# Exponentials of pairs of tiles in two places by turns, and weight blocks taken up two tiles behind their load: a fused attention and feed-forward kernel on one core

## The chip, the cores and the metric

The kernel runs on one core of a Trainium2 chip. A core has five engines that run side by side and wait for each other by semaphores: TensorE (PE in the profile; its weight loads are PEld), VectorE (DVE), ScalarE (ACT), GpSimd (POOL) and SyncE (SP), which here issues all transfers. Each engine works through its instructions in a fixed order. The metric is the device time of one launch in microseconds; the kernel before took 1450.28 us (median of three runs, 1449.85 to 1451.96).

## The reference

```python
scores = scale * np.matmul(q, k.transpose(0, 1, 3, 2))          # q, k, v: (8, 8, 576, 64)
thresh = np.max(scores, axis=-1, keepdims=True) - tau
scores = np.where(scores >= thresh, scores, -1000000000.0)
attn = np.exp(scores - np.max(scores, axis=-1, keepdims=True))
attn = attn / (np.sum(attn, axis=-1, keepdims=True) + 1e-09)
x = np.matmul(attn, v)                                           # -> (4608, 512), heads side by side
h = x @ w_in                                                     # w_in (512, 2048)
g = np.maximum(h, 0.0) + np.log1p(np.exp(-np.abs(h)))            # softplus
out = g @ w_out                                                  # w_out (2048, 512)
```

All inputs are 32-bit floats, tau is a scalar of 0.02.

## The kernel before

**Attention in units of nine tiles.** A unit is a pair of heads of one batch: 32 units, of 2 x 576 = 1152 query rows each. Its nine tiles have 128 queries by 576 keys: tiles 0 to 3 are of the first head, 5 to 8 of the second, and tile 4 (called M or `NC` in the code) takes 64 rows of each. For one tile PE makes the scores in one of two pairs of PSUM banks (`scores`, line 423); DVE takes the row maximum, negated (`row_max`, line 430), and a threshold (line 431); ACT writes the exponentials to SBUF (`exps`, line 435); DVE puts zeros where the score is under the threshold and sums the rows (`mask`, line 440); PE transposes the result (`weights_T`, lines 471, 474, 477); ACT copies the transposes to gH (`weights_hi`, lines 498 to 514); and PE multiplies them with v (`values`, lines 549 to 557).

**The place of the exponentials.** They stand in `e_all`, of two halves of 576 columns, which tiles use by turns through the whole program (`nth[0] % 2`). 576 is four blocks of 128 and a rest of 64. Tiles go in pairs, 0 and 1, 2 and 3, 5 and 6, 7 and 8 (`mate`), with tile 4 alone; at the second of a pair one transpose, line 471, takes the rests of both tiles at once, the last 64 columns of the left half and the first 64 of the right half. Line 474 has the four blocks, line 477 the rest of the lone tile.

**The first units and the rest.** The first five units (`NF`, `whole`) multiply with v in full 32-bit products and have no low parts of the weights, so the buffers of tag gL stand unused there; the others split the weights in a high part gH and a low part gL. For the first 36 tiles (`TG`) transposes go to PSUM banks of their own, and the steps of a tile stand in the order `PAT0`, later in the order `PAT`, with letters for row maximum (R), exponential (e), mask (M or m), transposes (T), copies (h, l), scores (S), FFN products (f), weight blocks (w), other steps (x, v) and a count (p). `p` stands twice in each, so a tile counts two points, and `defer(n, ...)` puts a step off by n points. This order is a priority: a scheduler sets each engine's order from it and from a model of when inputs will be there, so instructions can stand earlier or later than the letters say.

**The feed-forward part (FFN).** Nine chunks of 512 tokens follow behind attention: `hidden` (lines 645, 647, 649), softplus on ACT, `project` (lines 703, 705, 707). Its first chunk needs the output of the first units, so the first 36 tiles have no FFN products beside them; after that they are strewn between the steps of attention.

**The weight blocks.** Each of 32 blocks of w_in and w_out is loaded once (SP, line 185), as words of 64 bits from which a 32-bit float is put together: an absolute value with a scale on ACT (line 193), a clamp on POOL (line 194), a shift and two "or"s on DVE (lines 200, 202, 205), and a high and a low part on POOL (lines 125, 132); parts of w_in are stored to DRAM again (SP, line 234). A block begins every second tile from tile 1. `later_(WD, first)` puts ACT's step off by WD points from the load.

Of the kernel before, what the change touches and what calls it, by code (L numbers as in the profile page):

```python
# [9 lines left out]
F32 = mybir.dt.float32  # L10
F32R = mybir.dt.float32r
# [12 lines left out]
P = 128  # L24
# [8 lines left out]
LAG0 = 5  # L33
PAT = "ThRlefmpfxSvwp"
PAT0 = "RMTeShlfpfxvwp"
WD = 2
ST = (1, 3, 4, 4, 5, 6, 6, 8)
VO = (1, 1, 1, 0)
RT = 1
# [20 lines left out]
def tile_kernel(ctx: ExitStack, tc: tile.TileContext, q, k, v, tau, w_in, w_out, out):  # L60
# [8 lines left out]
    nc = tc.nc  # L69
    B, H, S, D = q.shape  # L70
    NT, DM = out.shape
    DFF = w_in.shape[1]
    SM = 512
    SR = S - SM
    HS = S // 2
    NC = SM // P
# [8 lines left out]
    apool = ctx.enter_context(tc.tile_pool(name="apool", bufs=2))  # L85
# [11 lines left out]
    ident = identr.bitcast(F32)  # L97
# [52 lines left out]
    def to_f32(src, want, name, then):  # L150
# [29 lines left out]
        if src.dtype == F32:  # L180
            nc.sync.dma_start(m, src)
            later_(WD, lambda: then(parts, w, done))
            return
# [29 lines left out]

        later_(WD, first)

# [59 lines left out]
    for b in range(B):  # L275
        for kind in (("one", "two") if b < NSPLIT else ("all",)):
            for hp in range(NPAIR):
                s = Unit()
# [5 lines left out]
                for g, (j, members) in enumerate(groups):  # L284
                    c = 0
# [113 lines left out]

    e_all = cpool.tile([P, 2, S], F32, name="e_all")
    banks = [ps_s.tile([P, 2, 512], F32, tag="s", name=f"s_{i}") for i in range(SB)]
    nth = [0]

    def scores(s, t):
        if t == s.tiles[0]:
            s.sums = apool.tile([P, 9], F32, tag="sums", name=f"sums_{s.i}")
            s.half, s.sp, s.m, s.grp = {}, {}, {}, {}
        sp = banks[nth[0] % SB]  # L410
        s.half[t] = half = nth[0] % 2
        nth[0] += 1
        s.sp[t] = sp
        if t == NC:
            parts = [(qm[:, n, j, :], j) for j in range(2) for n in range(2)]
        else:
            j = 0 if t < NC else 1
            c = t if t < NC else t - NC - 1
            parts = [(s.qT[j][n][:, c * P:(c + 1) * P], j) for n in range(2)]
        k0 = (1 - half) * SR  # L420
        for m, (lhs, j) in enumerate(parts):
            for hf in range(2):
                i = nc.tensor.matmul(sp[:, hf, 0:HS], lhs, s.kT[j][:, k0 + hf * HS:k0 + (hf + 1) * HS],  # L423
                                     start=(m == 0), stop=(m == len(parts) - 1))
        scored.append(i)
# [6 lines left out]
        s.m[t] = (negm, thr)  # L432

    def exps(s, t):
        nc.scalar.activation(e_all[:, s.half[t], :].rearrange("p (h n) -> p h n", h=2), s.sp[t][:, :, 0:HS],  # L435
                             AF.Exp, bias=s.m[t][0], scale=1.0)

    def mask(s, t):
        e2 = e_all[:, s.half[t], :].rearrange("p (h n) -> p h n", h=2)
        masked.append(nc.vector.scalar_tensor_tensor(  # L440
            out=e2, in0=s.sp[t][:, :, 0:HS], scalar=s.m.pop(t)[1], in1=e2, op0=ALU.is_ge, op1=ALU.mult,
            accum_out=s.sums[:, s.tiles.index(t):s.tiles.index(t) + 1]))
# [8 lines left out]
    def mate(s, t):  # L451

        if t == NC:
            return None, False
        u = t if t < NC else t - 1
        return (t + 1, False) if u % 2 == 0 else (t - 1, True)

    def weights_T(s, t):
        half = s.half[t]
        e = e_all[:, half, :]  # L460
        other, second = mate(s, t)
        lone = other is None
        if 9 * NPAIR * s.b + 9 * s.hp + t < TG:
            main = ps_g.tile([P, NC, P], F32, tag="g", name=f"tm_{s.i}_{t}")
            rest = ps_g.tile([P, NC, P], F32, tag="g", name=f"tr_{s.i}_{t}")[:, 0, :] if lone or second else None
        else:
            sp = s.sp[t]
            main = sp[:, 0, :].rearrange("p (c n) -> p c n", n=P)
            rest = sp[:, 1, 0:P]
        if second:  # L470
            nc.tensor.transpose(rest, e_all.rearrange("p h n -> p (h n)")[:, SM:SM + P], ident)  # L471
        for c in range(NC):
            c0 = half * SR + c * P
            nc.tensor.matmul(main[:, c, :], e[:, c0:c0 + P], ident, is_transpose=True, start=True, stop=True)  # L474
        if lone:
            r0 = 0 if half else SM
            nc.tensor.transpose(rest[0:SR, :], e[:, r0:r0 + SR], ident)
        s.sp[t] = (main, rest)
# [358 lines left out]
    for kind, g in WL:  # L837
        for m in range(4):
            n = len(prep)
# [71 lines left out]
    for n in (0, 2, 1):  # L911
        qkT(u0, 1, n)
        point()
    u0.eng, u0.eng_lo = eng, nc.gpsimd
    scores(*tiles[0])
    row_max(*tiles[0])
    exps(*tiles[0])
    scores(*tiles[1])
    for j in range(2):
        split_v(u0, j)  # L920
# [3 lines left out]
    for g, (cur, t) in enumerate(tiles):  # L924
# [5 lines left out]
        for step in PAT0 + ("m" if g == TG - 1 else "") if g < TG else PAT:  # L930
            if step == "T":
                weights_T(cur, t)
            elif step == "h":
                weights_hi(cur, t)
            elif step == "l":
                weights_lo(cur, t)
            elif step == "R" and nxt:
                row_max(*nxt)
            elif step == "e" and nxt:
                exps(*nxt)  # L940
            elif step == "m" and nxt:
                mask(*nxt)
            elif step == "M":
                mask(cur, t)
            elif step == "f":
                upto += quota / PAT.count("f")
                while done < upto:
                    done += next(ffn)
            elif step == "x":
                extras(cur.i, cur.tiles.index(t))  # L950
            elif step == "S" and g + 2 < NS:
                scores(*tiles[g + 2])
            elif step == "v":
                slow_products()
            elif step == "w":
                while prep and prep[0][0] <= g:
                    _, f, a = prep.pop(0)
                    f(*a)
            elif step == "p":
                point()  # L960
# [38 lines left out]
```

## Time and profile before

| | |
|---|---|
| median of 3 runs | 1450.28 us (1449.85 to 1451.96) |
| the profiled execution | 1450.65 us, span 1448.9 us |
| PE busy | 1399.3 us, 97% of the span |
| DVE busy | 983.1 us, 68% |
| ACT busy | 848.1 us, 59% |
| POOL busy | 591.0 us, 41% |
| mean granted PE clock | 0.994 |

The shares are means over stages that differ: PE is not full in the first tenth of the span and almost full after it. An engine's idle time is written beside the instruction that came after it, with what ended it. Idle time on an engine that nobody waits for costs nothing.

### The profile page before, as it was taken

What the parts mean: (1) busy time and instruction counts of PE and PEld (TensorE: products, weight loads), DVE (VectorE), ACT (ScalarE), POOL (GpSimd) and SP (SyncE); (2) the same over time, 40 slices, a digit from 0 to 9 for tenths busy, and PEclk for the clock granted to TensorE, in tenths of its full rate; (3) what the DMA queues carried; (4) which work ended last, traced back from release to release, by engine and by line L of the source; (5) the groups of instructions that cost most, each with busy time, mean ns of one, the idle gap of its engine ahead of it and who ended that gap; (6) DMA issues with size and microseconds to landing.
All of it is one profiled execution on the core that took longest, in us unless ns stands there. A gap on an engine that the chain in (4) does not pass through costs nothing.

```text
span 1448.9 us, 23497 instructions
## 1 busy us (share of the span) xinstructions
PE 1399.3 (97%) x7860; PEld 1161.6 (80%) x7860; DVE 983.1 (68%) x2211; ACT 848.1 (59%) x1615; POOL 591.0 (41%) x619
## 2 busy tenths in 40 slices
PE   6987999999999999999999999999999999999998
PEld 4654788878888888888888888888888888788886
DVE  6977688877777777777777777777777777402111
ACT  5766767767656566657665665667665765311010
POOL 3667666544333333344334333444334431324221
PEclk9999999999999999999999999999999999999999
DMA  5767765445333533444433533354344532344321
GB/s 160 220 192 231 212 187 170 138 121 154 109 102 110 137 115 110 119 134 150 123 111 96 153 106 101 116 151 120 113 119 136 148 98 74 101 130 129 119 85 44
DMA packets 131208, 189.93 MB, mean 131 GB/s; under 512 B 35312, under 2 KB 86800, under 8 KB 131088
## 3 DMA queue, kind: packets, MB, share of 16 engines
q1 hardware_dynamic: 131088, 188.43, 44.5%
q8 instruction: 63, 1.03, 0.3%
q14 instruction: 57, 0.47, 0.1%
HBM read 140.51 MB, written 27.41 MB: 116 GB/s over the span
## 4 chain that ended last, share of the span: by engine, by line
PE 78%; DVE 7%; ACT 5%; issue 3%; DMA 3%; POOL 2%; SPq 1%; POOLq 0%; ACTq 0%; DVEq 0%
PE s L423 10%; PE h L647 9%; PE h L645 9%; PE h L649 8%; PE o L707 8%; PE o L705 7%; PE s L474 7%; PE o L703 7%; PE pv L555 3%; PE pv L556 3%; PE tr L364 2%; DVE e_all L440 2%; DVE negm L430 2%; PE pv L549 1%; POOL g L132 1%
## 5 line engine op out<-in xcount | busy, mean ns | idle before, releaser
L132 POOL TENSOR_TENSOR g<-st,g 128x512 fp32r<-128x512 f32 x144 | 191.7, 1349 | 196.3 <-DVE g L129 182.5
L440 DVE SCALAR_TENSOR_TENSOR e_all<-s,thr,e_all 128x576 f32<-128x576 f32 x288 | 234.4, 815 | 53.0 <-ACT e_all L435 49.8
L430 DVE TENSOR_REDUCE negm<-s 128x1 f32<-128x576 f32 x288 | 217.1, 754 | 43.1 <-PE s L423 34.6
L435 ACT ACTIVATE e_all<-s,negm 128x576 f32<-128x576 f32 x288 | 215.9, 751 | 39.3 <-PE tr L471 20.7
L707 PE MATMUL o<-wo_o,g 128*128 128x512 f32 x576 | 232.3, 404 | 5.3 <-POOL g L132 5.3
L703 PE MATMUL o<-wo_o,g 128*128 128x512 f32 x576 | 232.0, 403 | 1.1 <-ACT st L667 0.7
L647 PE MATMUL h<-xl,wi 128*128 128x512 f32 x576 | 232.8, 404 | 0.0
L645 PE MATMUL h<-xh,wi 128*128 128x512 f32 x576 | 229.8, 399 | 0.0
L649 PE MATMUL h<-xh,wi 128*128 128x512 f32 x576 | 229.3, 398 | 0.0
L705 PE MATMUL o<-wo_o,g 128*128 128x512 f32 x576 | 228.5, 397 | 0.0
L498 ACT CAST gH<-s 128x512 fp32r<-128x512 f32 (+1 forms) x270 | 145.0, 550 | 139.1 <-PE s L474 135.6
L132 DVE TENSOR_TENSOR gL<-s,gH 128x512 fp32r<-128x512 f32 (+1 forms) x270 | 168.8, 634 | 47.8 <-ACT gH L498 25.3
L423 PE MATMUL s<-kT,qT 128*128 128x288 f32 x1024 | 192.2, 310 | 6.2 <-ACT gH L498 1.8
L423 PEld LDWEIGHTS s<-kT,qT 128*128 128x128 f32 x1024 | 148.5, 190 | 27.9 <-issue 11.3
L474 PE MATMUL s<-identr,e_all 128*128 128x128 f32 x1008 | 155.1, 276 | 4.8 <-DVE e_all L440 4.8
L129 DVE CAST g<-st 128x512 fp32r<-128x512 f32 x128 | 57.4, 485 | 149.5 <-ACT st L667 149.0
L667 ACT ACTIVATE st<-h 128x512 f32<-128x512 f32 x144 | 78.3, 596 | 115.3 <-PE h L649 114.6
L474 PEld LDWEIGHTS s<-identr,e_all 128*128 128x128 f32 x1008 | 114.7, 141 | 22.3 <-DVE e_all L440 12.6
L707 PEld LDWEIGHTS o<-wo_o,g 128*128 128x128 f32 x576 | 108.4, 188 | 29.1 <-POOL g L132 11.0
L645 PEld LDWEIGHTS h<-xh,wi 128*128 128x128 f32 x576 | 108.3, 188 | 23.5 <-issue 1.0
L703 PEld LDWEIGHTS o<-wo_o,g 128*128 128x128 f32 x576 | 108.5, 188 | 22.2 <-DVE g L129 2.0
L649 PEld LDWEIGHTS h<-xh,wi 128*128 128x128 f32 x576 | 108.4, 188 | 21.6
(107 smaller groups left out, 2366.4 us busy)
## 6 DMA issues: line engine op xcount, KB each, us to landing
wi<-wi_d SPq DMA_DIRECT2D x144, 512.0 KB
qT<-qT SPq DMA_DIRECT2D x124, 128.0 KB
R<-r_d SPq DMA_DIRECT2D x64, 144.0 KB
kn<-in_k_dram SPq DMA_DIRECT2D x32, 256.0 KB
qn<-in_q_dram SPq DMA_DIRECT2D x32, 256.0 KB
vn<-in_v_dram SPq DMA_DIRECT2D x32, 256.0 KB
wc_i<-in_moe_w_in_dram SPq DMA_DIRECT2D x16, 512.0 KB
wi_d<-wc_i SPq DMA_DIRECT2D x32, 256.0 KB
```

The costliest lines, as they stand in the source:

```text
L132: eng.tensor_tensor(out=out_, in0=in_, in1=hi.bitcast(F32), op=ALU.subtract)
L423: i = nc.tensor.matmul(sp[:, hf, 0:HS], lhs, s.kT[j][:, k0 + hf * HS:k0 + (hf + 1) * HS], start=(m == 0), stop=(m == len(parts) - 1))
L430: nc.vector.reduce_max(negm, s.sp[t][:, :, 0:HS], axis=AX.XY, negate=True)
L435: nc.scalar.activation(e_all[:, s.half[t], :].rearrange("p (h n) -> p h n", h=2), s.sp[t][:, :, 0:HS], AF.Exp, bias=s.m[t][0], scale=1.0)
L440: masked.append(nc.vector.scalar_tensor_tensor(out=e2, in0=s.sp[t][:, :, 0:HS], scalar=s.m.pop(t)[1], in1=e2, op0=ALU.is_ge, op1=ALU.mult, ...
L474: nc.tensor.matmul(main[:, c, :], e[:, c0:c0 + P], ident, is_transpose=True, start=True, stop=True)
L645: nc.tensor.matmul(h, wi[:, 0, cc, :], u.h[cc], start=(cc == 0), stop=False)
L647: nc.tensor.matmul(h, wi[:, 0, cc, :], u.l[cc], start=False, stop=False)
L649: nc.tensor.matmul(h, wi[:, 1, cc, :], u.h[cc], start=False, stop=(cc == NCC - 1))
L703: nc.tensor.matmul(o, gh[:, sl], wo[fc][:, 0, :], start=(i == 0), stop=False)
L705: nc.tensor.matmul(o, gh[:, sl], wo[fc][:, 1, :], start=False, stop=False)
L707: nc.tensor.matmul(o, gl[:, sl], wo[fc][:, 0, :], start=False, stop=(i == QF - 1))
```

## The change

A second place for exponentials, `e_more`, is laid over a buffer of tag gL, which the first five units don't use. In these units pairs (and the lone tile) take `e_more` and `e_all` by turns; from unit 5 on all take `e_all`. The half is no longer taken by turns through the program: the first of a pair and the lone tile take the left one, the second of a pair the right one. And WD goes from 2 points to 4.

```diff
-WD = 2
+WD = 4
...
     e_all = cpool.tile([P, 2, S], F32, name="e_all")
+    e_more = apool.tile([P, NC, 320], F32R, tag="gL", name="e_more").bitcast(F32)
+    e_more = e_more.rearrange("p c n -> p (c n)")[:, 0:2 * S].rearrange("p (h n) -> p h n", h=2)
+    pairs = [0]
...
         sp = banks[nth[0] % SB]
-        s.half[t] = half = nth[0] % 2
+        half = s.half[t] = int(mate(s, t)[1])
+        pairs[0] += not half
+        s.e[t] = e_more if s.whole and pairs[0] % 2 else e_all
         nth[0] += 1
...
     def exps(s, t):
-        nc.scalar.activation(e_all[:, s.half[t], :].rearrange("p (h n) -> p h n", h=2), s.sp[t][:, :, 0:HS],
+        nc.scalar.activation(s.e[t][:, s.half[t], :].rearrange("p (h n) -> p h n", h=2), s.sp[t][:, :, 0:HS],
...
     def mask(s, t):
-        e2 = e_all[:, s.half[t], :].rearrange("p (h n) -> p h n", h=2)
+        e2 = s.e[t][:, s.half[t], :].rearrange("p (h n) -> p h n", h=2)
...
     def weights_T(s, t):
         half = s.half[t]
-        e = e_all[:, half, :]
+        e = s.e[t][:, half, :]
...
         if second:
-            nc.tensor.transpose(rest, e_all.rearrange("p h n -> p (h n)")[:, SM:SM + P], ident)
+            nc.tensor.transpose(rest, s.e[t].rearrange("p h n -> p (h n)")[:, SM:SM + P], ident)
```

Lines of the changed kernel have numbers that are 6 higher from `e_all` on (441 is `exps`, 477 the transpose of rests). The scheduler's order changes in units 0 to 8, and later at a few places of every fourth unit. Three of them follow; in names the numbers are those of unit and tile (negm_1_3: unit 1, tile 3), and the last one is the buffer's.

ACT in unit 1, around the exponentials of tiles 3 and 4 and the third block of w_in's second group (wa_i1_2); before:

```order
L582 COPY rt_0_601<-rT_0_590 9x128
L551 COPY xp_0_302<-pv_0_3_560 64x256
L193 ACTIVATE wa_i1_2_720<-wc_i1_2_719 128x512
L435 ACTIVATE e_all_141<-s_0_142,negm_1_3_608 128x576
L498 COPY gH_1_1_627<-tm_1_2_613 128x4x128
L512 ACTIVATE gH_1_1_627<-tr_1_3_647,side_102 128x128
L435 ACTIVATE e_all_141<-s_1_143,negm_1_4_641 128x576
```

And changed:

```order
L588 COPY rt_0_596<-rT_0_588 9x128
L557 COPY xp_0_301<-pv_0_3_555 64x256
L441 ACTIVATE e_more_142<-s_0_143,negm_1_3_603 128x576
L504 COPY gH_1_1_622<-tm_1_2_608 128x4x128
L193 ACTIVATE wa_i1_2_715<-wc_i1_2_714 128x512
L441 ACTIVATE e_all_141<-s_1_144,negm_1_4_639 128x576
L518 ACTIVATE gH_1_1_622<-tr_1_3_645,side_102 128x128
```

The weight block moved from ahead of tile 3's exponential to behind it, and tile 4's exponential, now in another place than tile 3's, moved ahead of a copy of the rest transpose of tile 3.

PE in unit 4, where FFN products (h) begin; before:

```order
L471 MATMUL s_1_143<-identr_81,e_all_141 128x128
L474 MATMUL s_1_143<-identr_81,e_all_141 128x128 x4
L364 MATMUL tr_5_0_0_1674<-identr_81,k2_5_1604 128x128 x4
L645 MATMUL h_0_0_1739<-xh_0_0_1715,wi_0_0_1733 128x512
L647 MATMUL h_0_0_1739<-xl_0_0_1716,wi_0_0_1733 128x512
```

And changed:

```order
L477 MATMUL s_1_144<-identr_81,e_all_141 128x128
L480 MATMUL s_1_144<-identr_81,e_all_141 128x128 x4
L364 MATMUL tr_5_0_0_1671<-identr_81,k2_5_1599 128x128 x4
L480 MATMUL s_0_143<-identr_81,e_more_142 128x128 x4
L483 MATMUL s_0_143<-identr_81,e_more_142 64x128
L429 MATMUL s_1_144<-kT_4_1_1458,qT0_4_1_1464 128x288 x2
L429 MATMUL s_1_144<-kT_4_1_1458,qT1_4_1_1465 128x288 x2
L555 MATMUL pv_4_0_1638<-gH_4_0_1562,vn_4_1207 64x256 x2
L429 MATMUL s_0_143<-kT_4_1_1458,qT0_4_1_1464 128x288 x2
L429 MATMUL s_0_143<-kT_4_1_1458,qT1_4_1_1465 128x288 x2
L480 MATMUL s_1_144<-identr_81,e_all_141 128x128 x4
L651 MATMUL h_0_0_1737<-xh_0_0_1713,wi_0_0_1731 128x512
```

The first FFN product moved behind the transposes of tiles 4 and 5 and the scores between them.

ACT in unit 9, between the exponentials of tiles 4 and 5; before:

```order
L435 ACTIVATE e_all_141<-s_1_143,negm_9_4_4051 128x576
L368 CAST kT_10_0_4088<-tr_10_0_0_4083 128x512
L435 ACTIVATE e_all_141<-s_0_142,negm_9_5_4113 128x576
L390 CAST kT_10_0_4088<-tr_10_0_2_4141 128x2x64
L396 ACTIVATE qm_107<-tr_10_0_2_4141,qscale_88 128x64 x2
```

And changed:

```order
L441 ACTIVATE e_all_141<-s_1_144,negm_9_4_4052 128x576
L368 CAST kT_10_0_4089<-tr_10_0_0_4084 128x512
L390 CAST kT_10_0_4089<-tr_10_0_2_4142 128x2x64
L396 ACTIVATE qm_107<-tr_10_0_2_4142,qscale_88 128x64 x2
L504 CAST gH_9_1_4001<-s_1_144 128x4x64
L504 CAST gH_9_2_4109<-s_1_144 128x4x64
L516 CAST gH_9_1_4001<-s_1_144 64x64
L516 CAST gH_9_2_4109<-s_1_144 64x64
L441 ACTIVATE e_all_141<-s_0_143,negm_9_5_4114 128x576
```

Tile 5's exponential moved behind the copies of tile 4's transposes, since both tiles now use the left half of `e_all`.

## Rows read from the trace of the kernel before

**Rows 1.** Busy time of each engine by stretch (us); PEclk is the granted clock.
```profile
core 0: us, PE busy (x) PEld busy (x) DVE busy (x) ACT busy (x) POOL busy (x), PEclk, DMA share, GB/s
14.00:50.00 36.00, 30.31 (x167) 21.92 (x168) 29.08 (x65) 23.60 (x54) 18.21 (x24) 0.95 0.69 202
50.00:80.00 30.00, 26.27 (x154) 17.65 (x153) 26.74 (x56) 20.98 (x48) 18.53 (x23) 1.00 0.80 222
80.00:110.00 30.00, 25.70 (x144) 16.95 (x143) 23.24 (x54) 20.01 (x47) 20.31 (x23) 0.94 0.63 177
110.00:146.00 36.00, 28.05 (x148) 18.69 (x146) 26.70 (x52) 22.50 (x51) 27.34 (x32) 0.91 0.73 220
800.00:1000.00 200.00, 198.39 (x1180) 170.38 (x1179) 149.94 (x346) 131.94 (x243) 78.33 (x82) 1.00 0.45 129
```

**Rows 2.** The chain of waits, 15 to 160 us, shares by line.
```profile
by line: issue 12.1%; PE pv L549 11.2%; DMA wc_i<-in_moe_w_in_dram 10.0%; PE s L423 7.0%; DVE e_all L440 6.9%; DVE negm L430 5.5%; DMA wc_o<-in_moe_w_out_dram 3.9%; DVE wa_i L205 3.3%; ACT gH L498 3.1%; DMA wi_d<-wc_i 3.1%; ACT e_all L435 3
```

**Rows 3.** ACT's groups, 14 to 146 us: count, busy us, mean ns, idle before.
```profile
L435 ACT ACTIVATE e_all<-s,negm 128x576 f32<-128x576 f32 x40 | 30.0, 749 | 26.3 <-PE tr L471 20.7 <-PE s L471 3.9 <-DVE negm L430 1.5
L498 ACT COPY gH<-tm 128x512 f32<-128x512 f32 (+1 forms) x40 | 21.2, 541 | 1.2 <-PE tm L474 0.9
...
L193 ACT ACTIVATE wa_i<-wc_i 128x512 f32<-128x512 f32 x12 | 8.2, 681 | 11.0 <-DMA wc_i<-in_moe_w_in_dram 11.0
...
L193 ACT ACTIVATE wa_o<-wc_o 128x512 f32<-128x512 f32 x7 | 4.7, 675 | 2.9 <-DMA wc_o<-in_moe_w_out_dram 2.9
```

**Rows 4.** PE's groups, 14 to 146 us.
```profile
L474 PE MATMUL tm<-identr,e_all 128*128 128x128 f32 x144 | 23.4, 287 | 10.6 <-DVE e_all L440 7.0 <-DVE thr L431 3.5
...
L471 PE MATMUL tr<-identr,e_all 128*128 128x128 f32 x16 | 5.3, 328 | 6.3 <-DVE e_all L440 3.8 <-DVE thr L431 2.5
```

**Rows 5.** DVE's groups, 14 to 146 us.
```profile
L440 DVE SCALAR_TENSOR_TENSOR e_all<-s,thr,e_all 128x576 f32<-128x576 f32 x40 | 32.4, 811 | 11.6 <-ACT e_all L435 11.5
...
L200 DVE TENSOR_SCALAR wa_o<-wa_o 128x512 uint32<-128x512 uint32 x7 | 4.0, 577 | 6.1 <-POOL wa_o L194 6.1
```

**Rows 6.** Timeline of DVE, row maxima: start us, length us.
```profile
24.56 0.76 DVE L430 TENSOR_REDUCE negm<-s 128x1 f32<-128x576 f32 x1
...
60.34 0.74 DVE L430 TENSOR_REDUCE negm<-s 128x1 f32<-128x576 f32 x1
...
70.10 0.75 DVE L430 TENSOR_REDUCE negm<-s 128x1 f32<-128x576 f32 x1
...
142.23 0.76 DVE L430 TENSOR_REDUCE negm<-s 128x1 f32<-128x576 f32 x1 [0.52 <-PE s L423]
```

**Rows 7.** Timeline of ACT; idle time before, and what ended it, in brackets.
```profile
27.16 0.74 ACT L435 ACTIVATE e_all<-s,negm 128x576 f32<-128x576 f32 x1 [2.57 <-PE tr L471]
...
50.89 0.67 ACT L193 ACTIVATE wa_i<-wc_i 128x512 f32<-128x512 f32 x1 [1.78 <-DMA wc_i<-in_moe_w_in_dram]
...
62.30 0.74 ACT L435 ACTIVATE e_all<-s,negm 128x576 f32<-128x576 f32 x1 [2.15 <-PE tr L471]
...
71.27 0.74 ACT L435 ACTIVATE e_all<-s,negm 128x576 f32<-128x576 f32 x1
...
132.38 0.68 ACT L193 ACTIVATE wa_o<-wc_o 128x512 f32<-128x512 f32 x1 [1.91 <-DMA wc_o<-in_moe_w_out_dram]
...
145.32 0.74 ACT L435 ACTIVATE e_all<-s,negm 128x576 f32<-128x576 f32 x1 [3.94 <-PE s L471]
```

**Rows 8.** Timeline of PE.
```profile
105.52 1.30 PE L423 MATMUL s<-kT,qm 128*128 128x288 f32 x8
...
139.84 2.29 PE L423 MATMUL s<-kT,qm 128*128 128x288 f32 x8 [2.71 <-ACT gH L498]
...
146.16 0.47 PE L645 MATMUL h<-xh,wi 128*128 128x512 f32 x1
```

**Rows 9.** The first "or" on DVE, 14 to 146 us: ns min/median/max.
```profile
L202 DVE SCALAR_TENSOR_TENSOR wa_i<-wc_i,wa_i x12: 676/970/1623, 23.8 to 119.2; 128x512 uint32<-128x512 uint32 x12
L202 DVE SCALAR_TENSOR_TENSOR wa_o<-wc_o,wa_o x6: 680/688/952, 76.3 to 137.2; 128x512 uint32<-128x512 uint32 x6
```

More of the change, by code (lines that the diff above doesn't have):

```diff
@@ L408, in scores @@
             s.sums = apool.tile([P, 9], F32, tag="sums", name=f"sums_{s.i}")
-            s.half, s.sp, s.m, s.grp = {}, {}, {}, {}
+            s.half, s.sp, s.m, s.grp, s.e = {}, {}, {}, {}, {}
         sp = banks[nth[0] % SB]
-        s.half[t] = half = nth[0] % 2
+        half = s.half[t] = int(mate(s, t)[1])
+        pairs[0] += not half
+        s.e[t] = e_more if s.whole and pairs[0] % 2 else e_all
         nth[0] += 1
```

## The prediction

> **What bounds the kernel now.** I read the table by stretches of time first. From 14 to 146 us TensorE (PE) is busy for 30.31 + 26.27 + 25.70 + 28.05 = 110.3 of 132 us (84%) and VectorE (DVE) for 29.08 + 26.74 + 23.24 + 26.70 = 105.8 us (80%); neither is full. Between 800 and 1000 us PE is busy for 198.39 of 200 us [rows 1]. So there are two programs in one: a first stretch, in which 40 tiles of attention [rows 3] have no feed-forward (FFN) products beside them and go as fast as their chain of waits lets them, and a long rest, whose length is PE's work. What the first stretch saves, the end saves, one for one; what is saved on another engine in the rest is worth nothing.
>
> Next the chain of waits, of 15 to 160 us: no engine has more than a fraction of it; loads of w_in blocks hold 10.0% and of w_out blocks 3.9% [rows 2]. Then the groups by engine. ScalarE (ACT) stands idle before the exponentials for 26.3 us, 20.7 of it until a transpose of line 471 is done, and before taking up weight blocks for 11.0 + 2.9 us, until their loads land [rows 3]. On the other side PE is idle for 10.6 + 6.3 us before the transposes that read the masked exponentials [rows 4], and DVE for 11.6 us before the mask, nearly all until the exponential is there, and 6.1 us before the first shift of w_out blocks [rows 5]. That is a ring: exponential, mask, transpose, next exponential.
>
> **Part 1, two places for pairs.** In e_all the second tile's rest transpose (line 471) reads 64 columns of both halves, so the exponential of the next pair's first tile, which writes one of them, must wait for it. After the change that tile writes the other place. What comes last for it then is its own row maximum. At 62.30 an exponential waits 2.15 us, but its maximum was ready at 60.34 + 0.74 = 61.08: 1.22 us late, not 2.15. Where no transpose is waited for, the distance is between 0.03 and 0.42 us, as at 71.27 (70.10 + 0.75 = 70.85, 0.42 later) [rows 6, 7]; I take 0.2. There are 13 such exponentials, the first at 27.16 (24.56 + 0.76 = 25.32, 1.84 late), the last at 145.32 (142.23 + 0.76 = 142.99, 2.33 late) [rows 6, 7]; their 13 distances add up to 17.1 us, less 13 x 0.2 = 14.5 us. This is the most that this part can take out of the ring.
>
> The price: no instruction and no memory is added, since the second place lies in a buffer that these five units don't use. But from unit 5 on there is one place, and tiles 4 and 5 now share a half, where they alternated; the exponential of tile 5 must wait for tile 4's transposes. ACT's copies of those transposes (0.541 us each [rows 3]) stood ahead of that exponential in most units already; in eight (5, 8, 9, 13 and every fourth from there) it moves behind four copies and some small casts, about 4 x 0.541 = 2 us. I cost this at nothing: FFN products fill PE there, 198.39 of 200 us [rows 1]. Were that cover gone, it would be 8 x 2 = 16 us.
>
> **Part 2, weight blocks taken up later.** The order on ACT shows that WD = 4 does less than its number says: of the first 18 blocks nine stand behind the same exponential as before, and only the other nine move back, by one exponential or two. Four of the nine loads that ACT waited for are among the moved: the first at 50.89 (1.78 us), the last at 132.38 (1.91 us) [rows 7], 7.1 us together. The other 6.8 of 13.9 us stay. The four are part of the ring only by the exponential behind them; measured by its distance to its own maximum, three of these add 1.8 + 1.5 + 0.5 = 3.8 us less 0.1 (the fourth is counted in part 1): 3.7 us. Stores of finished blocks now stand behind the swaps of q on SP, and some loads of k behind loads of weights; they are used tiles later, and I cost them at nothing, the first because it lets q come earlier, the second because nine tiles lie between.
>
> **The sum.** Both parts together take at most 14.5 + 3.7 = 18.2 us out of the ring. What is late next? DVE and PE themselves. In the densest part, 50 to 80 us, DVE is busy for 26.74 of 30 us (89%) and PE for 26.27 (88%) [rows 1]. If the whole stretch became as dense as that, by DVE it would last 105.8 / 0.891 = 118.7 us (13.3 saved), by PE 110.3 / 0.876 = 126.0 us (6.0 saved). The mean is 9.6 us, and half of 18.2 is 9.1; I take 9.1. Against it stands one loss that the order on PE shows: the first FFN product, at 146.16 [rows 8], comes behind two more tiles of attention. A tile takes 132 / 40 = 3.3 us, and PE is idle for 22% of it (28.05 of 36 us busy [rows 1]): 2 x 3.3 x 0.22 = 1.5 us. So 9.1 - 1.5 = 7.6 us less. The profiled execution took 1450.65 us (span 1448.9 and 1.75 around it), 0.37 above the median of 1450.28; 1450.65 - 7.6 = 1443.05, and in terms of the median 1442.7 us.
>
> **A clock that could give more.** PE's granted clock was 0.95, 0.94 and 0.91 in three of the four parts, so it was at the lower of its two levels (1.2, not 2.4 GHz) for some 10% of 36, 12% of 30 and 18% of 36 us (a mean of 0.95 over levels of 0.5 and 1 is a tenth at the lower): 13.7 us. The product of line 423 that takes 1.30 us for eight at 105.52 takes 2.29 us at 139.84, right after PE had stood idle for 2.71 us [rows 1, 8]. Fewer such gaps mean fewer slow stretches: at most half of that, 6.8 us. I count none of it in the forecast, and it is why the low side is the longer one.
>
> **The rivals.**
> *More than that.* If the ring was all that held the tiles, all 18.2 us go, less 1.5: 1450.3 - 16.7 = 1433.6 us. Against it: PE would be busy for 110.3 of 115 us without FFN products between, and no part of the stretch comes near. For it: the clock. Chance 0.12.
>
> *The unmoved loads take over.* Nine blocks stay right before an exponential. If exponentials come 0.9 us sooner each and those loads land no sooner, up to 9 x 0.9 = 8.1 of the 18.2 us turn into waits for loads; half of the remaining 10.1, less 1.5, is 3.6: 1446.7 us. Against it: the loads are issued by SP behind work that also comes sooner. Chance 0.12.
>
> *DVE and GpSimd (POOL) get in each other's way.* The "or" of line 202 takes 676 ns at best and 1623 at worst for w_in blocks, 680 to 952 for w_out ones, same shape [rows 9]. If closer packing brings all 18 from the median to the longest, that is 12 x 0.65 + 6 x 0.26 = 9.4 us more on DVE, and the gain is gone: 1450.3 - 7.6 + 9.4 = 1452 us; at half of that, 1447.4. The Trainium skill ("SBUF — State Buffer", "Who interferes with whom") speaks against this change here: a VectorE instruction with two SBUF inputs and a GpSimd instruction that reads SBUF lock each other out for a whole instruction; the spread from 676 to 1623 ns agrees with that, and by that rule the time lies at the upper of these two numbers. But both engines do the same work as before, and DVE's order now puts the mask ahead of the weight's shift in most places, so the delay falls on work that is not in the ring. Chance 0.12 for about no change, by this or by any wait that takes the place of the removed ones.
>
> *Slower: FFN products start late.* PE's order is fixed. If tiles 4 and 5 of unit 4 come no sooner than now, PE waits where it had products to do: up to both tiles, 2 x 3.3 = 6.6 us. It decides as soon as the first 36 tiles save less than that; with 2 us saved the time is 1450.3 - 2 + 6.6 = 1454.9 us. For it: PE's longest gaps lie just there, 2.71 us at 139.84 and the 3.94 us that ACT waits at 145.32 [rows 7, 8]. Against it: attention alone keeps PE busy for most of these tiles. Chance 0.12.
>
> **How the numbers follow.** The forecast has 0.52; its own range is 1437 to 1447 us. Down to 1433 it takes in nearly all of the first rival, up to 1452 the second and third; what is left out is the slower case and a little at the low end, some 0.15 to 0.2. A difference under 0.2% (2.9 us) is not told from no change. Faster by more: 0.52 + 0.12 + most of 0.12, less a little, 0.72; within 0.2%: 0.16; slower: 0.12.
>
> **What would show it.** Right: no exponential of units 0 to 4 waits for a rest transpose; the first FFN product comes some 4 to 10 us before 146; DVE's idle time before the mask falls from 11.6 to under 6 us; the rest of the trace is as long as before. ACT's wait for loads falls to about 7 us; at 14 or more the second rival is right. The or of line 202 at a median over 1.3 us would be the third. A hole of some us in PE just before the first FFN product would be the last. The forecast is wrong if the first product comes no sooner than 146, or if units 5 to 31 take longer than they did.

## The result and the profile after

The changed kernel took 1457.02 us (median of 5 runs, 1455.9 to 1458.24); beside it the kernel before took 1450.23 (5 runs, 1449.38 to 1451.96). The ratio is 1.0047, with a 95% interval from 1.0033 to 1.0062: slower, by 6.8 us. The profiled execution took 1458.13 us, with a span of 1456.3. Most single executions lie within 3 us of their kernel's median, a few up to 6 away, and each trace is one of them (those of e1 and e6 below lie 4 us above their median, those of e4 and e11 2 us under it); so what follows leans on differences that come back in several kernels. Two executions, one of e7 (2558 us) and one of the kernel before (2070 us), ran in a slow state and are in no time below.

The table by stretches, whose counterpart is [rows 1]:

```profile
core 0: us, PE busy (x) PEld busy (x) DVE busy (x) ACT busy (x) POOL busy (x), PEclk, DMA share, GB/s
14.00:50.00 36.00, 29.33 (x170) 21.42 (x170) 29.64 (x66) 25.32 (x56) 16.47 (x22) 1.00 0.66 193
50.00:80.00 30.00, 28.37 (x166) 19.16 (x166) 28.70 (x60) 22.11 (x52) 21.09 (x25) 1.00 0.83 230
80.00:110.00 30.00, 26.46 (x163) 18.68 (x163) 27.52 (x58) 22.81 (x57) 21.11 (x25) 1.00 0.69 205
110.00:146.00 36.00, 27.94 (x143) 18.07 (x142) 26.28 (x52) 22.75 (x50) 25.70 (x31) 0.92 0.63 179
146.00:190.00 44.00, 40.02 (x202) 28.88 (x202) 24.48 (x51) 29.65 (x53) 27.07 (x28) 0.99 0.77 234
190.00:235.00 45.00, 41.88 (x243) 34.54 (x242) 40.83 (x80) 30.31 (x60) 26.70 (x29) 1.00 0.61 183
235.00:290.00 55.00, 52.43 (x301) 43.37 (x300) 46.94 (x104) 40.98 (x79) 32.34 (x37) 0.97 0.48 136
```

The first stretch did get denser: PE does 499 matmuls from 14 to 110 us instead of 465, and its clock stays at the higher level there. The loss lies behind it, from 146 to 290 us, a stretch that the prediction did not look at. PE is idle there for 144 - 134.33 = 9.7 us, against 3.2 before, and its clock is granted at less than full for part of it: 0.01 x 44 + 0.03 x 55 = 2.1 us of full speed.

One product that occurs once in each of the 32 units, the one that writes rT, serves as a milestone. It stands at the second tile of the unit that follows, so the stretch between the milestones of units 5 and 6, called unit 5 below, holds tiles of unit 6. Its start, in us after (+) or before (-) its start in the trace of the kernel before:

| unit (start before) | 2 (103.89) | 3 (133.28) | 4 (179.97) | 5 (221.22) | 6 (260.86) | 7 (299.24) | 31 (1244.12) |
|---|---|---|---|---|---|---|---|
| after | -4.8 | -3.7 | -2.7 | +0.8 | +3.4 | +4.0 | +7.5 |

So there are three parts: 4.8 us won by unit 2, 8.7 lost from unit 2 to 7, and 3.5 more lost, bit by bit, from unit 7 to the end.

**The first stretch.** ACT's groups of 14 to 146 us (columns as in [rows 3]):

```profile
L441 ACT ACTIVATE e_all<-s,negm 128x576 f32<-128x576 f32 x22 | 16.4, 747 | 7.7 <-DVE negm L436 7.6
L441 ACT ACTIVATE e_more<-s,negm 128x576 f32<-128x576 f32 x20 | 14.9, 744 | 12.1 <-DVE negm L436 12.0
...
L193 ACT ACTIVATE wa_i<-wc_i 128x512 f32<-128x512 f32 x12 | 8.2, 686 | 9.5 <-DMA wc_i<-in_moe_w_in_dram 9.5
```

The waits for rest transposes, 24.6 us of the 26.3 in [rows 3], are gone. In their place ACT waits 7.6 + 12.0 = 19.6 us for the row maximum, where it was 1.5. The wait has changed its releaser and lost a quarter of its length.

DVE's groups of the same stretch, with the mask in its two places and the first "or" on w_out blocks, answer to [rows 5, 9]; idle time before the mask is 7.1 + 2.8 = 9.9 us, where it was 11.6:

```profile
L446 DVE SCALAR_TENSOR_TENSOR e_all<-s,thr,e_all 128x576 f32<-128x576 f32 x21 | 17.1, 812 | 7.1 <-ACT e_all L441 6.6
L446 DVE SCALAR_TENSOR_TENSOR e_more<-s,thr,e_more 128x576 f32<-128x576 f32 x21 | 17.0, 813 | 2.8 <-ACT e_more L441 2.2
...
L202 DVE SCALAR_TENSOR_TENSOR wa_o<-wc_o,wa_o 128x512 uint32<-128x512 uint32 x7 | 9.3, 1335 | 0.0
```

**From 146 to 290 us.** The first FFN product starts at 143.87 (146.16 in [rows 8]). PE's timeline; idle time before, and what ended it, in brackets:

```profile
134.40 1.32 PE L429 MATMUL s<-kT,qm 128*128 128x288 f32 x8 [1.68 <-ACT gH L504]
141.81 0.79 PE L429 MATMUL s<-kT,qT 128*128 128x288 f32 x4 [0.94 <-ACT gH L520]
143.87 0.78 PE L651 MATMUL h<-xh,wi 128*128 128x512 f32 x1
...
151.29 0.50 PE L653 MATMUL h<-xl,wi 128*128 128x512 f32 x1 [0.85 <-POOL xl L132]
...
154.07 0.73 PE L651 MATMUL h<-xh,wi 128*128 128x512 f32 x2 [0.79 <-ACT xh L127]
...
189.11 0.77 PE L429 MATMUL s<-kT,qT 128*128 128x288 f32 x4 [1.68 <-DVE gH L132]
...
231.78 0.40 PE L709 MATMUL o<-wo_o,g 128*128 128x512 f32 x1
...
235.93 0.54 PE L364 MATMUL tr<-identr,q 128*128 128x128 f32 x4 [0.68 <-DVE acc L726]
236.95 0.79 PE L429 MATMUL s<-kT,qT 128*128 128x288 f32 x4 [0.48 <-DVE gH L132]
239.05 0.74 PE L709 MATMUL o<-wo_o,g 128*128 128x512 f32 x1 [0.58 <-ACT st L673]
240.43 0.63 PE L709 MATMUL o<-wo_o,g 128*128 128x512 f32 x1
```

Around 134 and 143 the holes are no larger than before. New are four holes from 149 to 156, 2.3 us together, two of them shown; one at 189; five of 0.5 to 0.8 us from 197 to 219, 2.7 us, not shown (0.8 before); and a run of three at 236 to 239. In the first group the FFN products, which begin 2.3 us sooner, wait for their own input: ACT's cast of the first chunk's x (xh) at 153.40 has itself waited 2.87 us for the load of x, and POOL's low part (xl) follows. The kernel before has no such wait. After the last three, the same product takes 0.63 instead of 0.40 us: the clock has fallen. Behind the hole at 189, ACT at 186.08 waits 2.67 us for the load of a w_in block, with its gH, DVE's and then the PE row above behind it; the kernel before has a cast of w_in at 185.96 that waits for nothing. Ahead of the three stands this on ACT:

```profile
186.08 0.67 ACT L193 ACTIVATE wa_i<-wc_i 128x512 f32<-128x512 f32 x1 [2.67 <-DMA wc_i<-in_moe_w_in_dram]
...
234.68 0.65 ACT L504 CAST gH<-s 128x256 fp32r<-128x256 f32 x2 [2.01 <-PE s L483]
...
235.43 0.74 ACT L441 ACTIVATE e_all<-s,negm 128x576 f32<-128x576 f32 x1
...
236.41 0.67 ACT L193 ACTIVATE ws_o<-wc_o 128x512 f32<-128x512 f32 x1
237.10 1.28 ACT L673 ACT_TABLE_LOAD   x1
238.40 1.09 ACT L673 ACTIVATE st<-h 128x512 f32<-128x512 f32 x2
```

and this on DVE, where the five steps of two w_out blocks follow each other without a gap, ahead of the next row maximum:

```profile
238.52 0.43 DVE L200 TENSOR_SCALAR ws_o<-ws_o 128x512 uint32<-128x512 uint32 x1 [0.76 <-POOL ws_o L194]
238.86 0.69 DVE L202 SCALAR_TENSOR_TENSOR wa_o<-wc_o,wa_o 128x512 uint32<-128x512 uint32 x1
239.46 0.69 DVE L202 SCALAR_TENSOR_TENSOR ws_o<-wc_o,ws_o 128x512 uint32<-128x512 uint32 x1
240.06 0.68 DVE L205 SCALAR_TENSOR_TENSOR wa_o<-wc_o,wa_o 128x512 uint32<-128x512 uint32 x1
240.66 1.78 DVE L205 SCALAR_TENSOR_TENSOR ws_o<-wc_o,ws_o 128x512 uint32<-128x512 uint32 x1
242.37 0.74 DVE L436 TENSOR_REDUCE negm<-s 128x1 f32<-128x576 f32 x1
```

The softplus (table load and st) comes right behind the cast of the block ws_o. That cast, one exponential later than before, now stands behind casts that wait 2.01 us for PE. In the kernel before the order was the other way round:

```profile
231.62 0.69 ACT L193 ACTIVATE ws_o<-wc_o 128x512 f32<-128x512 f32 x1 [0.77 <-DMA wc_o<-in_moe_w_out_dram]
232.32 1.28 ACT L667 ACT_TABLE_LOAD   x1
233.62 1.09 ACT L667 ACTIVATE st<-h 128x512 f32<-128x512 f32 x2
234.59 0.66 ACT L498 CAST gH<-s 128x256 fp32r<-128x256 f32 x2
```

The softplus begins 16.4 us into unit 5 where it was 12.4, and PE's o products wait for it (the hole at 239.05).

### The profile page after: what moved, and what is told of

Same layout as the page of the kernel before. It is cut to its first block, busy times and chain, and to the rows that moved or that the text cites. A ratio compares the mean times of both kernels' runs of the same rounds, so it can differ in the third digit from the quotient of the medians.

```text
span 1456.3 us, 23491 instructions
## 1 busy us (share of the span) xinstructions
PE 1400.5 (96%) x7860; PEld 1161.4 (80%) x7860; DVE 990.8 (68%) x2211; ACT 851.5 (58%) x1615; POOL 591.8 (41%) x619
## 4 chain that ended last, share of the span: by engine, by line
PE 73%; DVE 9%; ACT 6%; issue 4%; DMA 4%; POOL 3%; SPq 1%; ACTq 0%; POOLq 0%; DVEq 0%
PE s L429 10%; PE h L651 8%; PE h L653 8%; PE h L655 8%; PE o L713 7%; PE o L711 7%; PE s L480 7%; PE o L709 7%; PE pv L562 3%; PE pv L561 3%; DVE negm L436 2%; PE tr L364 2%; DVE e_all L446 2%; ACT st L673 2%; ACT L673 1%
## 5 line engine op out<-in xcount | busy, mean ns | idle before, releaser
L446 DVE SCALAR_TENSOR_TENSOR e_all<-s,thr,e_all 128x576 f32<-128x576 f32 x265 | 215.9, 816 | 37.5 <-ACT e_all L441 34.0
L441 ACT ACTIVATE e_all<-s,negm 128x576 f32<-128x576 f32 x265 | 198.8, 750 | 22.0 <-DVE negm L436 12.4
L480 PE MATMUL s<-identr,e_all 128*128 128x128 f32 x988 | 150.6, 275 | 5.4 <-DVE e_all L446 5.4
L651 PEld LDWEIGHTS h<-xh,wi 128*128 128x128 f32 x576 | 108.5, 188 | 25.4 <-ACT xh L127 2.1
L653 PEld LDWEIGHTS h<-xl,wi 128*128 128x128 f32 x576 | 108.6, 188 | 22.6 <-POOL xl L132 2.0
```

What stands on the lines that cost most here:

```text
L441: nc.scalar.activation(s.e[t][:, s.half[t], :].rearrange("p (h n) -> p h n", h=2), s.sp[t][:, :, 0:HS], AF.Exp, bias=s.m[t][0], scale=1.0)
L446: masked.append(nc.vector.scalar_tensor_tensor(out=e2, in0=s.sp[t][:, :, 0:HS], scalar=s.m.pop(t)[1], in1=e2, op0=ALU.is_ge, op1=ALU.mult, ...
L651: nc.tensor.matmul(h, wi[:, 0, cc, :], u.h[cc], start=(cc == 0), stop=False)
L653: nc.tensor.matmul(h, wi[:, 0, cc, :], u.l[cc], start=False, stop=False)
```

## The experiments

All times are medians of 5 to 12 runs, beside runs of the kernel before on the same chip (medians 1449.8 to 1450.7); in brackets the 95% interval of the ratio. The first four split the change. My theory, A in the texts on record, was that the two places bring the early gain, the late take-up loses more where the FFN begins, and the shared half costs a drift; its rival, B, puts the loss down to the places, with the numbers given there. One thing in these texts is wrong: WD counts points, of which a tile has two, so WD = 4 is two tiles and not four, WD = 2 is one and WD = 1 half a tile; and LAG0 moves the start of the FFN, not the tiles of the first unit.

**e1, the places alone**

```
-WD = 4
+WD = 2
```

> The two places with WD back at 2 points; all else as changed. Theory A (WD = 4 brings the loss of some 8 us between units 3 and 6, because weight work and the first feed-forward product come later; the two places save some 4.8 us in units 0 to 2; the half shared by tiles 4 and 5 costs some 2.9 us over units 11 to 31): 1450.2 - 4.8 + 2.9 = 1448 us, first feed-forward product near 141. Theory B (the places bring the loss, because tiles come sooner than x and the weights): about 1455 us, with idle gaps of PE at the start of the feed-forward part.

1456.53 us, ratio 1.0047 (1.0030 to 1.0065). That is near theory B's number, but not at its place: the table below has the loss by unit 3 and none from there to 7.

**e2, the late take-up alone:** the kernel before with

```
-WD = 2
+WD = 4
```

> WD = 4 alone, one place, halves by turns as before. Theory A: 1450.2 + 5 to 8 = 1455 to 1458 us, the first feed-forward product behind transposes of tiles 4 and 5 of unit 4, and no drift from unit 11 on. Theory B: 1447 to 1450 us, since four waits for loads go.

1456.48 us, 1.0044 (1.0029 to 1.0059), as theory A has it.

**e3, both without the shared half**

```
-        half = s.half[t] = int(mate(s, t)[1])
-        pairs[0] += not half
+        half = s.half[t] = nth[0] % 2
+        pairs[0] += not mate(s, t)[1]
```

> As changed (two places, WD = 4), but the half is taken by turns through the program again, so tiles 4 and 5 have different halves. If the shared half costs the drift from unit 11 on: 1457.0 - 2.9 = 1454 us, with the transposes of row sums of units 11 to 31 at a fixed distance from those of the kernel before. If the drift has another cause: 1457 us.

1454.03 us, 1.0027 (1.0017 to 1.0037): the drift goes, as forecast for a cost of the shared half.

**e4, the places alone without the shared half:** e3's edit and WD = 2.

> Two places, halves by turns, WD = 2: the part that should only gain. Theory A: 1450.2 - 4.8 = 1445 us. Theory B: some 1452 us, the loss between units 3 and 6 still there.

1454.44 us, 1.0027 (1.0017 to 1.0036): over both expectations.

So each part makes the kernel slower by itself, and their losses don't add. The milestones of these traces, as above:

| unit | 2 | 3 | 4 | 5 | 6 | 7 | 31 |
|---|---|---|---|---|---|---|---|
| e1 | +5.9 | +8.1 | +6.4 | +6.3 | +7.3 | +7.2 | +10.2 |
| e2 | -2.1 | -1.5 | +0.8 | +1.8 | +5.7 | +6.8 | +6.0 |
| e3 | -4.3 | -3.2 | -1.5 | +0.1 | +3.2 | +3.7 | +4.2 |
| e4 | +2.7 | +4.5 | +3.1 | +2.4 | +1.3 | +1.3 | +1.6 |

With WD = 4 the first stretch is faster and some 7 to 8 us are lost from unit 3 to 7; with WD = 2 nothing is lost there. That part of theory A holds. The other does not: with WD = 2 the second place makes the first stretch slower. DVE's timeline in e4 shows why:

```profile
80.08 1.50 DVE L200 TENSOR_SCALAR wa_o<-wa_o 128x512 uint32<-128x512 uint32 x1 [0.58 <-POOL wa_o L194]
81.50 0.74 DVE L436 TENSOR_REDUCE negm<-s 128x1 f32<-128x576 f32 x1
...
82.89 0.80 DVE L446 SCALAR_TENSOR_TENSOR e_more<-s,thr,e_more 128x576 f32<-128x576 f32 x1
```

ACT had written that e_more from 79.84 to 80.59; its mask starts 2.3 us after that, behind a shift that waited for POOL. From 75 to 110 us PE waits 8.2 us for masks in e4 and 1.0 in e3 (and 1.9 there for thresholds, the step before).

**e5, the shared half alone:** the kernel before, one place, with

```
-        s.half[t] = half = nth[0] % 2
+        s.half[t] = half = nth[0] % 2 if s.whole else int(mate(s, t)[1])
```

> The kernel before (one place, WD = 2) with one thing changed: from unit 5 on tiles 4 and 5 share the left half. If that costs the drift seen in the changed kernel from unit 11 on (2.9 us): 1450.5 + 2.5 to 4 = 1453 to 1454.5 us, the drift spread over the units in small steps. If the drift needs the two places: 1450.5 us.

1452.34 us, 1.0018 (1.0009 to 1.0027): about 2 us slower. From unit 7 to 31 its trace loses 2.6 us, in steps of about 0.4 at every fourth unit. The same steps (in the changed kernel +0.37 from unit 8 to 9, +0.42 from 12 to 13, +0.39 from 16 to 17) make most of the late loss wherever a half is shared: 3.5 us after, 2.9 in e1, 3.1 in e13; without, 0.5 in e3, 0.3 in e4, 0.0 in e14 (1.4 in e6, in two of the units and not by such steps). In such an interval of the changed kernel ACT has this:

```profile
685.99 0.74 ACT L441 ACTIVATE e_all<-s,negm 128x576 f32<-128x576 f32 x1 [0.85 <-PE s L477]
```

This is tile 7 of unit 17, and the kernel before waits 0.03 us at that place. Ahead of it tile 5's exponential begins 3.2 us behind tile 4's, where it was 1.1: the 2 us that the prediction saw. The loss per step, 0.4 us, is half of the wait.

The next four ask why the handover loses. H1: the first FFN product stands at another place in PE's order (row 220 before, 228 after). H2: the late blocks from the 17th on fall on engines that already serve the FFN.

**e6, e3's two places, with only the first 16 blocks late**

```
+        wd = WD if blocks[0] < 16 else 2
+        blocks[0] += 1
...
-        later_(WD, first)
+        later_(wd, first)
```

> Two places, halves by turns, WD = 4 for the first 16 weight blocks (those of the stretch that gains) and 2 for the last 16. Theory H1 (the loss between units 3 and 7 comes from the place of the first feed-forward product in PE's order, which is late here too, row 230 against 220 before): some 7 us lost there, 1453 to 1455 us. Theory H2 (it comes from the late weight blocks, which fall on GpSimd, ScalarE and VectorE when the feed-forward part begins): the loss goes, 1446 to 1447 us.

1449.87 us, 1.0004 (0.9995 to 1.0013): 4.2 us less than e3. From unit 3 to 7 it loses 1.2 us. Its first product stands in row 230, later than e3's, and the loss is gone: this speaks for H2, though the time is 3 us over H2's number.

**e7 and e8, e3 with the first FFN work started a tile earlier and a tile later**

```
-LAG0 = 5
+LAG0 = 4
```

> Two places, halves by turns, WD = 4, and the feed-forward stream begun one tile sooner (LAG0 = 4 for 5), which puts its first product at row 224 of PE's order instead of 228. H1: less of the loss between units 3 and 7, 1449 to 1452 us. H2: as with LAG0 = 5, 1454 us.

> The same with the feed-forward stream one tile later (LAG0 = 6), first product at row 239. H1: more of the loss, 1456 to 1459 us. H2: 1454 us.

LAG0 of 4, 5, 6 gives 1452.12 (1.0002 to 1.0020), 1454.03 (e3) and 1455.88 us (1.0028 to 1.0052). H1 seemed to have a part in it.

**e9, both at once:** e6 and LAG0 = 4.

> Two places with halves by turns, blocks taken up four tiles behind for the first 16 blocks and two behind after that, and the first unit's tiles started one earlier (LAG0 4). If late blocks and the place of the first FFN product are two separate losses that add, 1447 to 1448 us (1449.9 for the 16-block version less the 1.8 us that LAG0 4 gave with all blocks late). If both edits take away the same loss, about 1450 us.

1458.18 us, 1.0059 (1.0046 to 1.0072): a miss on both counts, the slowest kernel of all; from unit 3 to 7 it loses 11 us. H1 gives no rule: an earlier first product helped e3 by 1.9 us and cost e6 8.3.

**e10 and e11, the late take-up split by blocks, with one place:** e2 with wd = 4 only from the 17th block on, and only for the first 16.

> The kernel before with one place, blocks taken up two tiles behind for the first 16 and four behind for the rest; the first FFN product stands where it stood in PE's order before. If the late blocks at the handover are the loss (they fall on ScalarE, VectorE and GpSimd after the FFN has begun), 1454 to 1457 us with 4 to 7 us lost between units 3 and 7. If the place of the first FFN product is the loss, 1450 to 1451 us.

> The mirror of the run with the last blocks late: one place, the first 16 blocks taken up four tiles behind, the others two. If only the late blocks at the handover cost, 1448 to 1450 us, unit 2 about 2 us earlier than before and nothing lost from unit 3 to 7. If any late block costs at the FFN's start, 1452 to 1455 us.

e10: 1454.67 us, 1.0030 (1.0018 to 1.0041). e11: 1448.47 us, 0.9989 (0.9980 to 0.9998), the fastest that was run, 0.1% under the kernel before. As H2 has it: e10 leaves the first product where it was and loses 6 us from unit 3 to 7, e11 none.

**e12, e4 with DVE's shift put off** by two more points for the first 16 blocks; ACT takes them up as early as before.

```
-            later_(1, lambda: second(0))
+            later_(dv, lambda: second(0))
```

> Two places with halves by turns, all blocks taken up two tiles behind as before, but for the first 16 blocks VectorE's shift stands three points behind ScalarE's cast in place of one. If two places with blocks two behind lost its first stretch because a shift that waited for its load stood ahead of a mask in VectorE's order, unit 2 starts 2 to 5 us earlier than before and the time is 1449 to 1451 us. If it was ScalarE's own wait for the loads, unit 2 starts 2 to 4 us later than before and the time is 1453 to 1455 us.

1452.95 us, 1.0015 (1.0006 to 1.0024); unit 2 at +0.3. It lies between the two expectations: the shift ahead of the mask is part of e4's early loss, not all of it.

**e13, the changed kernel with only the last 16 blocks put back**

> The changed kernel with its two places and its shared half, and only the take-up of blocks 16 to 31 put back to two tiles. If the losses at the handover and by the shared half add, 1452 to 1453 us (1457.0 less the 4.2 us that the same edit took from the kernel with halves by turns). If the shared half costs only together with the late blocks, 1449 to 1450 us.

1450.38 us, 1.0002 (0.9991 to 1.0013). One edit takes back 6.5 of the 6.8 us (by the ratios). Its steps by the shared half are there all the same (2.8 us early at unit 7, 0.3 late at unit 31); what it wins before pays for them.

**e14 and e15, the last 16 split once more, one place:** late only blocks 16 to 23, and only 24 to 31.

> The kernel before with one place; only blocks 16 to 23 (taken up between about 120 and 185 us, while the first FFN products begin) wait for four tiles. If the hole in the unit that starts at 220 us is made by the blocks of that unit, no change: 1450 to 1451 us. If it is made by blocks left over from the time before, 1454 to 1456 us.

> The kernel before with one place; only blocks 24 to 31 (taken up between about 195 and 265 us) wait for four tiles. If they are what puts a waiting cast ahead of ScalarE's work for the FFN in the unit that starts at 220 us, 1453 to 1455 us with some 5 us lost in that unit. If the blocks before them are the cause, 1450 to 1451 us.

e14: 1448.94 us, 0.9989 (0.9981 to 0.9998). e15: 1454.18 us, 1.0024 (1.0015 to 1.0033). So most of the loss of late blocks comes with the last eight. Few of them even move in ACT's order: by the traces, 24 to 27 stand behind the same exponential in e15 as before, and 28, 29 and 31 behind the next one. Block 28 is the ws_o of the changed kernel above. ACT in e15, and in e13, where they are not late:

```profile
235.11 0.65 ACT L502 CAST gH<-s 128x256 fp32r<-128x256 f32 x2 [2.01 <-PE s L481]
...
237.48 0.69 ACT L197 ACTIVATE ws_o<-wc_o 128x512 f32<-128x512 f32 x1 [0.52 <-DMA wc_o<-in_moe_w_out_dram]
238.18 1.28 ACT L671 ACT_TABLE_LOAD   x1
239.48 1.09 ACT L671 ACTIVATE st<-h 128x512 f32<-128x512 f32 x2
```

```profile
229.29 1.28 ACT L677 ACT_TABLE_LOAD   x1
230.59 1.09 ACT L677 ACTIVATE st<-h 128x512 f32<-128x512 f32 x2
231.56 0.66 ACT L508 CAST gH<-s 128x256 fp32r<-128x256 f32 x2
```

In e13 the softplus stands ahead of the casts of gH, which then find PE done: the wait is gone. In e15 it stands behind. Unit 5 by milestones, changed kernel and e13, with the same number of matmuls:

```profile
222.04:264.30 42.26, 40.19 (x226) 33.24 (x225) 37.84 (x80) 27.88 (x54) 25.40 (x28) 0.96 0.48 140
```

```profile
218.33:258.06 39.73, 38.41 (x226) 31.93 (x225) 35.47 (x78) 27.94 (x53) 24.80 (x29) 1.00 0.50 154
```

Of the 2.5 us between them, 0.8 is idle time of PE and 1.8 are slower matmuls, at a mean clock of 0.96. But the lower clock is not what makes the unit long. e3 has the softplus as late (17.1 us), its clock stays at 1.00, and the same matmuls take as long with idle time in place of the longer matmuls:

```profile
221.29:264.05 42.76, 38.92 (x226) 32.10 (x225) 37.78 (x81) 27.64 (x53) 25.57 (x28) 1.00 0.46 139
```

At LAG0 = 5 all traces but one fall into two groups: softplus at 12.1 to 12.9 us into unit 5 and the unit 38.6 to 40.6 long (before, e1, e4, e5, e6, e11 to e14, e17, e18), or softplus at 16.4 to 17.9 and the unit 42.3 to 45.1 (after, e2, e3, e10, e15: those with the last eight blocks late).

**e16, earlier instead of later:** the first 16 blocks late, the last 16 only one point, half a tile, behind.

> One place, the first 16 blocks taken up four tiles behind their load and the last 16 only one tile behind. If later is worse at the handover because the work falls on busy engines, earlier could be better yet: 1445 to 1448 us. If the loads are then waited for, 1450 to 1453 us.

1456.17 us, 1.0033 (1.0020 to 1.0045). This is the one trace outside the groups: the softplus is in place (12.0) and unit 5 takes 43.5 us, with the clock at 1.00. Its largest hole on PE, 2.31 us, ends at 237.22 with a step of DVE that stands behind a w_out block's shift, and this shift has waited 2.05 us for POOL. So earlier does not help either, and it is not lateness as such that costs.

**e17 and e18, the first 24 blocks late,** with one place and with two (halves by turns).

> The kernel before with one place; the first 24 blocks taken up four tiles behind their load, the last eight two behind. Late blocks 0 to 15 gave -1.7 us and late blocks 16 to 23 gave -1.5: if these add, 1447 to 1448 us; if both take the same idle time, 1448.5 to 1449 us.

> The same with two places and halves by turns. If two places bring anything of their own once the last eight blocks stand as before and no half is shared, 1443 to 1446 us. If they only turn ScalarE's wait for the transpose into one for the row maximum, as with the first 16 blocks late, 1447 to 1450 us.

e17: 1453.08 us (1448.53 to 1457.03 over 11 runs), 1.0015 (1.0001 to 1.0029). e18: 1451.05 us, 1.0008 (0.9999 to 1.0017). Both expectations missed. Unit 5 is as short as before in both (40.0 us), but e17 loses 3.6 us from unit 3 to 4, and e18 1.8. In e17's trace this is the wait for x again, 3.12 + 0.52 us, as at 149 to 156 in the changed kernel; the longer of the two:

```profile
155.03 0.50 PE L649 MATMUL h<-xh,wi 128*128 128x512 f32 x1 [3.12 <-ACT xh L127]
```

e17's executions also fall into two groups: five of 1448.5 to 1450.5 us, with a mean granted clock of 0.997 to 0.999, and six of 1453.1 to 1457.0, at 0.996 to 0.997; the trace is of the second. Two gains of 1.5 us do not add, and no combination beats the kernel before by more than the 0.1% of e11 and e14. Beside e3, e18 has only the last eight blocks put back: 1451.05 for 1454.03 us, 2.8 us less by the ratios.

## Why the prediction was wrong

In the prediction's own terms, 9.1 us gained became 4.8, 1.5 us lost became 8.7, and a term put at nothing became 3.5: -4.8 + 8.7 + 3.5 = 7.4 us in the trace, where -7.6 was forecast.

**What bounds the kernel:** right for the rest, incomplete for the middle. It made two programs of the kernel, up to 146 us and from there. There is a third between: from 146 to 290 us the last dozen or so of the 32 blocks are converted while FFN products run, PE has little slack, and ACT's and DVE's order has a price. What was put at nothing there, since "a long rest, whose length is PE's work" begins at 146, is most of the miss.

**Part 1, at most 14.5 us out of the ring.** The waits went as forecast, but the step "what comes last then is its own row maximum", 0.2 us behind it, held for the releaser and not for the price: the maxima came later themselves. ACT's idle time before exponentials fell from 26.3 to 19.8 us, not by 14.5. And most of the gain by unit 2 is not the second place's. With the first blocks late it is 2.1, 2.5, 3.1 and 4.9 us with one place (e2, e16, e17, e11; mean 3.2), and 1.9 to 6.0 with two (eight traces; mean 4.5), a difference within the scatter of single executions; with no late blocks the second place loses (e1, e4). Two readings were a little off, without weight in the sum: at 105.96 the distance is 0.56 with no transpose waited for, and PE has a longer gap than 2.71 us, 3.62 at 16.36. The sign that was named for DVE, idle time before the mask under 6 us, was not met: 9.9.

**The shared half, costed at nothing.** Wrong by 2 to 3.5 us. The place and the delay of 2 us were right, the cover was not: with PE busy for 198.39 of 200 us, 0.4 us are still lost where ACT comes 0.85 late. The most it could be, 16 us, was far off.

**Part 2, 3.7 us.** ACT's waits for w_in loads fell from 11.0 to 9.5 us, those for w_out loads (2.9) are no longer among its waits. But only the first 18 blocks were looked at, those ahead of the first FFN product; the late take-up of the other 14 was put at nothing without a reason. This is the step that failed. With the last 16 put back (e13) the loss is gone; the last eight moved alone (e15) cost 3.8 us, and put back alone (e18 beside e3) they give back 2.8. The other 3.5 us that the changed kernel loses from unit 4 to 5, with the hole at 189, also go in e13; no run tests them by themselves. The block whose load is waited for there stands where it stood in ACT's order.

**Half of 18.2, 9.1 us.** By unit 2 it was 4.8, by unit 3 3.7, and the first FFN product came 2.3 us earlier, not 4 to 10. DVE was fuller than the sum allowed for: 28.70 of 30 us busy from 50 to 80.

**The FFN products two tiles later, 1.5 us.** The place was right, the mechanism was not. 8.7 us were lost from unit 2 to 7, most of it not by that: e15 leaves the first product where it was and loses 6 from unit 3 to 7. And the sooner product met a wait that the sum lacks: 2.3 us for the first chunk's x, 2.5 in e13's trace too and 3.6 in e17's. That is theory B's mechanism, but not by the places: with one place e2 has 2.2 us of it.

**The clock.** The lower level left 14 to 110 us, as was hoped for, and came back at 237 to 243, after three holes within 4 us (the sections on the experiments and on the hardware have e3, where such holes left it up):

```profile
237.00:240.00 3.00, 2.35 (x10) 1.71 (x11) 2.24 (x5) 2.97 (x6) 1.35 (x2) 0.86 0.27 81
240.00:243.00 3.00, 3.00 (x10) 2.44 (x9) 3.00 (x4) 2.98 (x5) 2.09 (x2) 0.57 0.65 170
```

**The rivals.** *More than that* did not come: 4.8 us by unit 2. *The unmoved loads take over*: not in the first stretch (9.5 us, with 14 as its sign), but one wait of 2.67 us at 186 is of that kind. *DVE and POOL*: its sign, a median over 1.3 us, was met for w_out blocks (1.46 us over 7, 0.69 before) and not for w_in ones (0.99); by the means, 7 x (1.34 - 0.73) = 4.3 us more on DVE. In each of the five of these "or"s (line 202) that took over 1.4 us from 14 to 146, a POOL instruction of lines 132 or 599 had begun up to 0.4 us before it, and it ended 0.55 us after that one. e3 has a median of 1.06 and e13 too; no run tests what it costs alone. *Slower*: the side was right, its mechanism wrong; there is no large hole just before the first FFN product. The time lies 2 us above its price of 1454.9.

**What stays open:** why late blocks 0 to 15 and 16 to 23 gain 1.5 us each but not together (e17), beyond the wait for x in one trace; why LAG0 = 4 turns its sign between e7 and e9; what lengthens unit 5 in e16, beyond the hole that is read from its one trace; and what makes the five holes from 197 to 219. What is shown is that the last eight blocks late cost, and the shared half; that the chain goes by the softplus' place is read from traces, where it comes back in five kernels, and was not moved by itself.

## What to carry to other kernels

A parameter that shifts work by some steps shifts all of it: follow the last instruction that it moves as closely as the first, above all where one phase hands over to the next, and look at what stands behind the moved instruction on its engine. A wait that is removed from a ring is worth what the next-latest releaser leaves, and that one moves too; ask when it will be ready, not when it was. Work that is brought forward can outrun its own input, as the first FFN products did with x. On an engine that is 99% busy a wait of 0.85 us elsewhere still cost 0.4, six times over.

## What the hardware showed unexpectedly

The same holes can lower the clock or leave it. Three holes of 0.5 to 0.7 us within 4 us (235.93 to 239.05) were followed in the changed kernel by a stretch in which the same product took 0.63 instead of 0.40 us. In e3 PE has the same three holes (0.68, 0.48 and 0.59 us, ending at 235.88, 236.90 and 239.00), ahead of the same products, and these go on at full clock:

```profile
240.00:243.00 3.00, 2.90 (x16) 2.25 (x14) 3.00 (x4) 2.98 (x5) 2.13 (x2) 1.00 0.61 168
```

In e9, with 13 us of idle time from 146 to 290, the granted clock stayed at 1.00 by the table of stretches, so idle time alone does not bring it down, and these runs do not show what does. Nor did the lower clock cost what it seemed to: unit 5 took 42.26 us with it and 42.76 in e3 without.
